# Batch 0's spatial product in three single-pass parts, with the opening's order written anew

## The chip, the cores and the metric

The kernel runs on one core of a Trainium2 chip. The metric is the device time of one execution in microseconds (us), the median of several. The core's engines run side by side, each through its own instructions in order: TensorE (in the profile PE, its weight loads PEld) multiplies matrices, VectorE (DVE) and ScalarE (ACT) work element by element, GpSimd (POOL) fills constants and issues a few transfers, SyncE (SP) issues nearly all transfers. An instruction waits at its engine's head until semaphores say that its operands are there and its target is free; everything behind it on that engine waits too.

## What is computed

Eight batches go through a linear attention with RMS norm, and its result through a gated block:

```python
kv = np.einsum('bhsd,bhse->bhde', k, v)            # B, H, S, D = 8, 8, 576, 64
out = np.einsum('bhsd,bhde->bhse', q, kv)
rms = np.sqrt(np.mean(out * out, axis=-1, keepdims=True) + 1e-06)
x = (out / rms * g_norm)                           # laid out as (B, 576, 512)
h = np.maximum(x @ w_in, 0.0)                      # w_in 512 x 1024
u, v = (h[..., :d_ff // 2], h[..., d_ff // 2:])
v_n = (v - mu) / np.sqrt(var + 1e-06)              # mean and variance over the 512 columns
v_s = np.einsum('ts,bsd->btd', w_spatial, v_n) + b_spatial[None, :, None]
return ((u * v_s) @ w_out).astype(np.float32)
```

All of it is in fp32. The product with `w_spatial` (576 x 576) is called the spatial product here.

## The kernel before

The 576 rows of a batch are four chunks of 128 (`NC`) and a tail of 64 (`TAIL`). Heads go in four pairs, so that a pair fills 128 partitions.

**Two ways to multiply.** A plain fp32 matmul is one instruction in the program and two records in the profile. From batch 1 on, an operand is held as a high part (a cast to fp32r by ScalarE) and a low part (the rest, a subtraction by VectorE); a product is then three fp32r matmuls, high by high, high by low, low by high (`hl`, `split`). Batches 1 to 7 also use seven products of quadrants instead of eight, for which sums of the quadrants of `w_spatial` lie ready in high and low parts (`WSH`, `WSL`, seven pieces for each of two row chunks).

**The opening.** Batch 0 starts while the weights still come in, and uses plain fp32: `hv_32` (v from `x` and `w_in`), `hv_tail_32` (the same for the tails of batches 0 and 1 together), `u_32` (u) and `sp_32`, the spatial product. `sp_32` makes eight units, four blocks of 128 columns by two halves of 288 rows; a unit sums over the four chunks and the tail, and VectorE multiplies the result into `U`. Meanwhile VectorE and ScalarE decode the float64 weights (`weight64_a` and `weight64_b`, five VectorE instructions for a 128x512 piece), split them (`split_in`, `split_ws`, `split_tail`, `split_out`), and TensorE already does batch 1's attention.

**What sets the order.** The string `PLAN` names the opening's steps, letter by letter: `W` the next weight load, `L` the next load of keys or queries, `c` and `C` the two halves of a decode, `J`, `K` the products of keys and values (instructions `pskv`), `A` and `D` queries (`pso`) and the norm's squares, `D` with ScalarE's accumulator, `A` with a VectorE reduction, `B` and `T` the norm's end and the transposes (`pstr`), `H` one step of `hv_32`, `e` and `F` relu and norm of v, `h` `hv_tail_32`, `u` u, `s` one unit of the spatial product, `X`, `E`, `z`, `O` the splits. Between `[` and `]` the order on PE, ACT and SP is pinned; behind that a scheduler orders the steps by its own timeline, in about the string's order. From the first `hv` of batch 1 (instructions `psh<-WVH,XH`) the program is written out in functions, `first`, `second` and `last` for each batch.

**Transfers.** SP issues in order; a transfer waits for the eighth before it, and for its buffer. Two key buffers (`KV0`, `KV1`) and two query buffers serve all pairs. The third and fourth piece of `w_out` come through one staging buffer: the third follows the stores of the first two split pieces (`spare_o<-WO`), the fourth the stores of the third.

Of the kernel before, what the change touches and what calls it, by code (L numbers as in the profile page):

```python
# [49 lines left out]
def body(ctx: ExitStack, tc, qT, kvm, kvt, g2, w_in, wsT, bsp, w_out, out):  # L50
# [275 lines left out]
    def split(hi, lo, x):  # L326
        nc.scalar.copy(hi, x)  # L327
        nc.vector.tensor_tensor(lo, x, f32(hi), op=ALU.subtract)  # L328
# [52 lines left out]
    def hv_tail_32():  # L381
        ps = ps_mm.tile([P, 512], F32, name="psh", tag="mm")
        for k in range(NP):
            nc.tensor.matmul(ps, X32[:, k, NT:XC], W32[k], start=k == 0, stop=k == NP - 1)
# [4 lines left out]
        d = work.tile([P, HS], F32, name="d", tag="g")[:, 0:HF]  # L389
        nc.vector.tensor_tensor(d[own], v[own, 0:HF], v[own, HF:FH], op=ALU.subtract)  # L390
        for x, cols in (v, slice(0, FH)), (d, slice(FH, FH + HF)):
            hi = TA[1][own, cols]
# [2 lines left out]
            nc.vector.tensor_tensor(TA[1][other, cols], x[own], f32(hi), op=ALU.subtract)

    def u_32(j, k):
        cols = slice(j * HS, (j + 1) * HS)
# [5 lines left out]
            if k == NP - 1:  # L404
                nc.scalar.activation(U[:, d, cols], psu[d], AF.Relu)

    def sp_32(d, j):
        ps = ps_mm.tile([P, 512], F32, name="psa", tag="mm")[:, 0:HS]
        ds, cols = slice(d * P, (d + 1) * P), slice(j * HS, (j + 1) * HS)
        for c in range(NC):  # L410
            nc.tensor.matmul(ps, V32[:, c, ds], staged["s", c][:, cols], start=c == 0, stop=False)  # L411
        nc.tensor.matmul(ps, VT32[0:TAIL + 1, ds], WT32[0:TAIL + 1, cols], start=False, stop=True)
# [334 lines left out]

    def blank_tails():
        nc.gpsimd.memset(VT32[TAIL:TAIL + 1], 1.0)
        for i in range(2):  # L750
            h = (1 - i) * TAIL
            nc.gpsimd.memset(f32(WTL[i][h:h + TAIL]), 0.0)
            nc.gpsimd.memset(f32(TB[i][h:h + TAIL]), 0.0)
            for r in (h, h + 32):
                nc.gpsimd.memset(f32(TB[i][r:r + 1, 0:FH]), 1.0)
# [267 lines left out]
```

## Time and profile before

| what | value |
|---|---|
| time, median of 3 runs (lowest to highest) | 512.27 us (512.09 to 512.9) |
| profiled execution: its time / its span | 511.49 us / 509.7 us |
| busy share of the span: PE, PEld, DVE, ACT, POOL | 98%, 86%, 81%, 57%, 4% |
| granted TensorE clock | 0.998 |
| DMA, mean over the span | 142 GB/s, 72.24 MB |

The span runs from the first to the last instruction. In rows of the timeline the first number is the start in us from the span's start, the second the duration of the row's whole group; `x8` counts instructions, and the bracket tells how long the engine had been idle and for whom it waited. Records of one engine overlap a little, since the next instruction starts while the last drains; the step from one start to the next is what an instruction costs in a dense stream. In rows of the chain of waits (the work that ended last, followed back) overlaps are taken off.

### The profile page before, as it was taken

The page shows a single profiled execution, that of the slowest core. Times are in us where ns is not written, and L with a number is a line of the kernel's source. Part 1 is how long each engine was busy: PE and PEld are TensorE (multiplying, and loading weights), DVE is VectorE, ACT ScalarE, POOL GpSimd, SP SyncE. Part 2 cuts the span into 40 slices and gives each one's busy share as a digit, 9 for nine tenths or more (in the row PEclk, how much of TensorE's full clock was granted, in tenths as well). Part 3 has the DMA queues.
Part 4 walks back from the last instruction along what each step waited for, and adds up shares of the span by engine and source line. Part 5 has one row for each costly group of instructions (what it writes and reads, how often), then busy time and mean ns, then how long its engine had stood idle before and what let it go on. Part 6 is the DMA issues. An engine that isn't in the chain of part 4 may idle for free.

```text
span 509.7 us, 9917 instructions
## 1 busy us (share of the span) xinstructions
PE 499.0 (98%) x3436; PEld 439.0 (86%) x3436; DVE 411.5 (81%) x1265; ACT 291.9 (57%) x1021; POOL 21.4 (4%) x47
## 2 busy tenths in 40 slices
PE   7999999999999999999999999999999999999996
PEld 6658788898988899989998899988998889988995
DVE  3898599688998699968897779968898579987860
ACT  2555456896734696457732688447642578527422
POOL 5000000000000001000000001000000001000000
PEclk9999999999999999999999999999999999999999
DMA  8995300735346516345265514424354511314223
GB/s 254 330 339 191 100 24 1 236 91 176 116 152 209 186 42 212 118 117 174 76 218 196 187 42 154 152 91 164 123 178 146 167 39 44 145 42 165 70 98 104
DMA packets 28071, 72.24 MB, mean 142 GB/s; under 512 B 3506, under 2 KB 8626, under 8 KB 26484
## 3 DMA queue, kind: packets, MB, share of 16 engines
q1 hardware_dynamic: 24564, 49.58, 29.9%
q0 software_dynamic: 3456, 22.02, 12.6%
q8 instruction: 27, 0.44, 0.4%
q14 instruction: 24, 0.20, 0.1%
HBM read 58.48 MB, written 13.11 MB: 140 GB/s over the span
## 4 chain that ended last, share of the span: by engine, by line
PE 78%; ACT 8%; DVE 7%; DMA 4%; POOL 1%; issue 1%; SPq 0%; ACTq 0%; POOLq 0%; DVEq 0%
PE pso L291 15%; PE psh L324 12%; PE psb L546 6%; PE psub L546 5%; PE pso L211 5%; PE psc L546 4%; PE pskv L136 3%; PE psa L546 3%; PE psua L546 3%; PE psuc L546 3%; PE psu L402 3%; PE psa L411 3%; PE psh L378 3%; PE pstr L239 2%; ACT x L194 2%; DMA out<-o 1%
## 5 line engine op out<-in xcount | busy, mean ns | idle before, releaser
L291 PE MATMUL pso<-WO,G 128*128 128x512 f32 x384 | 97.3, 396 | 0.0
L291 PEld LDWEIGHTS pso<-WO,G 128*128 128x128 f32 x384 | 70.3, 188 | 14.1
L327 ACT CAST G<-g 128x288 fp32r<-128x288 f32 (+1 forms) x56 | 22.8, 408 | 61.2 <-DVE g L567 60.8
L194 ACT ACTIVATE x<-pso 128x64 f32<-128x64 f32 x208 | 44.3, 252 | 5.5 <-PE pso L211 5.3
L324 PE MATMUL psh<-WVL,XH 128*128 128x512 f32 x112 | 43.7, 390 | 0.0
L324 PE MATMUL psh<-WVH,XH 128*128 128x512 f32 x112 | 43.6, 393 | 0.0
L194 ACT ACTIVATION_READ_ACCUMULATOR x<-pso 128x1 f32 x208 | 43.5, 238 | 0.0
L324 PE MATMUL psh<-WVH,XL 128*128 128x512 f32 x112 | 43.4, 392 | 0.0
L328 DVE TENSOR_TENSOR VL<-v,VH 128x512 fp32r<-128x512 f32 (+1 forms) x56 | 34.2, 619 | 7.8 <-ACT VH L327 7.6
L648 ACT COPY o<-pso 128x512 f32<-128x512 f32 x35 | 20.3, 593 | 26.0 <-PE pso L291 23.5
L327 ACT CAST VH<-v 128x512 fp32r<-128x512 f32 (+1 forms) x56 | 31.1, 574 | 4.2 <-DVE v L356 3.8
L303 DVE BATCH_NORM_STATS2 s<-v 128x6 f32<-128x512 f32 x32 | 21.8, 690 | 7.3 <-ACT v L297 7.1
L546 PE MATMUL psb<-WSH,VH 128*128 128x288 f32 x84 | 25.4, 304 | 0.2
L311 ACT ACTIVATE v<-v,mv,rv 128x512 f32<-128x512 f32 x28 | 23.2, 837 | 3.2 <-DVE mv L310 3.2
L324 PEld LDWEIGHTS psh<-WVH,XH 128*128 128x128 f32 x112 | 21.0, 188 | 4.6 <-ACT o L648 0.2
L297 ACT ACTIVATE v<-psh 128x512 f32<-128x512 f32 x32 | 18.7, 595 | 10.9 <-PE psh L324 7.6
L324 PEld LDWEIGHTS psh<-WVL,XH 128*128 128x128 f32 x112 | 21.0, 188 | 4.6
L324 PEld LDWEIGHTS psh<-WVH,XL 128*128 128x128 f32 x112 | 21.0, 188 | 4.4
L546 PE MATMUL psb<-WSL,VH 128*128 128x288 f32 x84 | 24.6, 295 | 0.0
L546 PE MATMUL psb<-WSH,VL 128*128 128x288 f32 x84 | 24.3, 297 | 0.1
L328 DVE TENSOR_TENSOR G<-g,G 128x288 fp32r<-128x288 f32 (+1 forms) x56 | 23.4, 418 | 1.1 <-ACT G L327 0.4
L136 PEld LDWEIGHTS pskv<-KV 128*64 128x64 f32 x512 | 18.1, 140 | 6.7 <-issue 2.9
(243 smaller groups left out, 1426.2 us busy)
## 6 DMA issues: line engine op xcount, KB each, us to landing
KV<-kvm SPq DMA_DIRECT2D x31, 512.0 KB, 5.1
WO<-spare_o POOLq DMA_DIRECT2D x12, 1024.0 KB, 6.6
UX<-spare_u POOLq DMA_DIRECT2D x12, 768.0 KB, 6.0
out<-o SPq DMA_DIRECT2D x32, 256.0 KB, 2.2
qt<-qT SPq DMA_DIRECT2D x16, 288.0 KB, 4.3
stage<-w_in SPq DMA_DIRECT2D x8, 512.0 KB, 6.4
qt<-qT SPq DMA_DIRECT2D x16, 256.0 KB, 2.9
KT<-kvt SPq DMA_DIRECT2D x32, 64.0 KB, 4.7
```

Of the source, the lines that this page charges most:

```text
L136: return nc.tensor.matmul(ps[h:h + D, at:at + D], of[:, 0, h:h + D], of[:, 1, h:h + D], start=c == 0, stop=c == NC)
L194: nc.scalar.activation(x[:, cols], ps[0:rows, cols], AF.Square, accum_out=ss[:, h:h + 1])
L211: nc.tensor.matmul(ps[:, c * P:(c + 1) * P], qt[:, c * P:(c + 1) * P], st[p], start=True, stop=True)
L291: nc.tensor.matmul(ps, lt, rh, start=i == 0, stop=i == n - 1)
L297: nc.scalar.activation(v, ps, AF.Relu)
L303: nc.vector.bn_stats(s6, v)
L311: nc.scalar.activation(v, v, AF.Identity, bias=m, scale=r)
L324: nc.tensor.matmul(ps, lt, rh, start=k == 0 and i == 0, stop=k == NP - 1 and i == 2)
L327: nc.scalar.copy(hi, x)
L328: nc.vector.tensor_tensor(lo, x, f32(hi), op=ALU.subtract)
L546: nc.tensor.matmul(ps, lt, rh, start=start and i == 0, stop=stop and i == len(pairs) - 1, skip_group_check=True)
L648: nc.scalar.copy(o, ps)
```

## The change

Batch 0's spatial product goes over to high and low parts. `sp_0` replaces `sp_32`: per chunk three fp32r matmuls with `WSH` and `WSL` instead of one in fp32, and the two matmuls of `tail_product` instead of one for the tail. `split_0` (letter `y`) splits the normalised v of batch 0, eight pieces of 128x256; `hv_tail_32` also splits batch 0's tail (`TA[0]`, `TB[0]`). The pieces of `w_spatial` must now be there before the units: `split_ws` (`E`) splits the four raw quadrants of a chunk pair, and the sums move behind the units, as `sums_ws` (`Y`); piece 6 holds a raw quadrant first and its sum later. One of the four norms of v multiplies on ScalarE (`f`). `PLAN` is new.

```diff
 PLAN = """
-[ W N8 G L c W C J00 L A00 L c L C n6 W J01 A01 J02 B00 T00 W A02 c H00 H20 J03 B01 T01 H30 B02 D03
-W T02 H31 c c W H10 C c W H11 H21 H32 H22 B03 H01 C c C W T03 H02 H12 H33 c H03 H13 L H23 e0 L | W C
-C L L a0 C e1 ] e2 e3 F1 L u00 F2 u01 K10 W Z F0 L A10 b0 L F3 t0 u02 u03 K12 u10 d1 b1 B10 A11 W
-u11 | | | t1 W u12 X3 W W A12 X2 Q0 h u13 s s L B12 T10 E0 s s B11 X0 E1 D13 s s X1 X5 W B13 T12 T11
-s X7 Q1 s T13 z P O1 p X4 X6 O0 W R
+[ L W N8 J00 L c G C D00 W n6 L W J01 c D01 B00 C J02 T00 L A02 H00 c B01 H30 H20 J03 T01 W B02 A03
+W T02 H10 W c c H31 C B03 L H21 L W H01 H22 C a0 H11 H32 C c H02 W W T03 C c H23 H33 H12 ] H03 e0
+H13 b0 L e1 C K10 F1 L L e2 W c e3 u00 C F2 f0 L t0 y1 y2 u01 F3 y0 A10 W K12 u02 X3 a1 Z u03 L y3
+u10 b1 X2 B10 t1 W A11 E0 u11 W L E1 W Q0 z u12 h D12 u13 s B12 s T10 X1 s | W s T12 X0 B11 D13 X5
+B13 s T11 X7 s s s Y1 Y0 X4 P T13 O0 Q1 W X6 p O1 R
 """
...
-        nc.scalar.copy(VT32[0:TAIL], v[0:TAIL])
-        own, other = slice(TAIL, P), slice(0, TAIL)
-        for x, cols in (v, slice(0, FH)), (d, slice(FH, FH + HF)):
-            hi = TA[1][own, cols]
+        for i, x, cols in (0, v, slice(0, FH)), (1, v, slice(0, FH)), (1, d, slice(FH, FH + HF)):
+            own, other = slice(i * TAIL, (i + 1) * TAIL), slice((1 - i) * TAIL, (2 - i) * TAIL)
+            hi = TA[i][own, cols]
             nc.scalar.copy(hi, x[own])
-            nc.scalar.copy(TB[1][own, cols], x[own])
-            nc.vector.tensor_tensor(TA[1][other, cols], x[own], f32(hi), op=ALU.subtract)
+            nc.scalar.copy(TB[i][own, cols], x[own])
+            nc.vector.tensor_tensor(TA[i][other, cols], x[own], f32(hi), op=ALU.subtract)
...
+    def split_0(c):
+        for i in range(2):
+            own = slice(i * HF, (i + 1) * HF)
+            name = ("p1", "u2", "u3", "g")[c]
+            hi0[c, i] = work.tile([P, HS], F32R, name=f"hi{name}", tag=name)[:, 0:HF]
+            split(hi0[c, i], V0L[:, c, own], raw[c][:, own])
...
-        for c in range(NC):
-            nc.tensor.matmul(ps, V32[:, c, ds], staged["s", c][:, cols], start=c == 0, stop=False)
-        nc.tensor.matmul(ps, VT32[0:TAIL + 1, ds], WT32[0:TAIL + 1, cols], start=False, stop=True)
+        cols, own = slice(j * HS, (j + 1) * HS), slice(d % 2 * P, (d % 2 + 1) * P)
+        multiply(ps, [m for c in range(NC) for m in
+                      hl(hi0[c, d // 2][:, own], V0L[:, c, d * P:(d + 1) * P],
+                         *(w[:, c % 2, (0, 6, 1, 2)[c // 2 * 2 + j]] for w in (WSH, WSL)))], True, False)
+        tail_product(ps, 0, d, j)
         nc.vector.tensor_tensor(U[:, d, cols], ps, U[:, d, cols], op=ALU.mult)
...
     def split_ws(k):
+        keep, b11, b12, b21, b22, _, _ = parts_ws(k)
+        for n, of in (0, b11), (1, b21), (2, b22), (6, b12):
+            keep(n, of)
+
+    def sums_ws(k):
+        keep, b11, b12, b21, b22, x, y = parts_ws(k)
         tc.keep_in_program_order(nc.vector.tensor_tensor(x, b12, b11, op=ALU.subtract))
         nc.vector.tensor_tensor(y, b22, x, op=ALU.subtract)
-        for n, of in enumerate((b11, b21, b22, x, y)):
-            keep(n, of)
+        keep(3, x)
+        keep(4, y)
```

Counted over the program, PE has 72 more matmuls of 128x288 (8 x 4 chunks x 3 and 8 x 2 tails instead of 8 x 5) and nothing else; behind the first `hv` of batch 1 its order is the same. DVE has eight more subtractions of 128x256, two of 128x288 and one of 64x512, and one reduction and one 128x512 scaling fewer. ACT has eight more casts of 128x256, two of 128x288, two of 64x512, and eight more squares of 128x64; one 64x512 copy is gone.

What moves, at three places. First SP at the program's start, before:

```order
L668 DMA stage<-w_in 128x1024
L900 DMA gcol<-g 128x1
L116 DMA KV_104<-kvm 128x2x256 x2
L117 DMA KT_106<-kvt 64x256
L126 DMA qt<-qT 128x576
```

and in the changed kernel:

```order
L115 DMA KV_104<-kvm 128x2x256 x2
L116 DMA KT_106<-kvt 64x256
L125 DMA qt<-qT 128x576
L682 DMA stage<-w_in 128x1024
L115 DMA KV_105<-kvm 128x1024
```

The first keys go ahead of the first weights. Second, PE where the spatial product begins (`psa` is a unit's bank, `pso` a query product, `psh<-RL,RH` the tails' v, `pstr` transposes of batch 1), before:

```order
L249 MATMUL pstt<-ident,x 128x128 x4
L211 MATMUL pso<-KVO_103,qt 128x128 x4
L384 MATMUL psh<-RL,RH 128x512 x4
L411 MATMUL psa<-stage,V_123 128x288 x8
L239 MATMUL pstr<-ident,x 128x128 x4
```

and in the changed kernel:

```order
L210 MATMUL pso<-KVO_102,qt 128x128 x4
L210 MATMUL pso<-KVO_103,qt 128x128 x4
L383 MATMUL psh<-RL,RH 128x512 x4
L238 MATMUL pstr<-ident,x 128x128 x4
L560 MATMUL psa<-WSH,hip_599 128x288
L560 MATMUL psa<-WSL,hip_599 128x288
```

The units now read `WSH`, `WSL`, the high parts `hi...` and `V0L` in place of the raw `stage` and `V`; batch 1's last query product and two groups of transposes, which lay among the units, follow them. Third, DVE ahead of the norms of batch 1's v (`BN_STATS`), before:

```order
L708 TENSOR_TENSOR WSL<-stage,WSH 128x288
L328 TENSOR_TENSOR WO<-stage,WO 128x512
L708 TENSOR_TENSOR WUL<-RL,WUH 128x2x256
L708 TENSOR_TENSOR WUL<-RL,WUH 128x512
L328 TENSOR_TENSOR WO<-stage,WO 128x512
L233 SCALAR_TENSOR_TENSOR XL<-pstr,gcol,XH 128x512
L762 TENSOR_TENSOR WTL_87<-WT_124,WTH 64x576
```

and in the changed kernel:

```order
L232 SCALAR_TENSOR_TENSOR XL<-pstr,gcol,XH 128x512
L722 TENSOR_TENSOR WSL<-stage,WSH 128x288
L152 COPY KVB<-pskv 64x2x64
L766 TENSOR_TENSOR stage<-stage 128x288
L722 TENSOR_TENSOR WSL<-stage,WSH 128x288
L722 TENSOR_TENSOR WUL<-RL,WUH 128x2x256
L327 TENSOR_TENSOR WO<-stage,WO 128x512 x2
```

The first two pieces of `w_out` are split last, behind the last of batch 1's x (`XL`) and the sums; the tails of `w_spatial` (`WTL`, `WTH`) are split early, before the units.

More of the change, by code (lines that the diff above doesn't have):

```diff
@@ L386, in hv_tail_32, with relu_0 @@
         layer_norm(ps, v, nc.vector)
-        nc.scalar.copy(VT32[0:TAIL], v[0:TAIL])
-        own, other = slice(TAIL, P), slice(0, TAIL)
-        d = work.tile([P, HS], F32, name="d", tag="g")[:, 0:HF]
-        nc.vector.tensor_tensor(d[own], v[own, 0:HF], v[own, HF:FH], op=ALU.subtract)
-        for x, cols in (v, slice(0, FH)), (d, slice(FH, FH + HF)):
-            hi = TA[1][own, cols]
-            nc.scalar.copy(hi, x[own])
-            nc.scalar.copy(TB[1][own, cols], x[own])
-            nc.vector.tensor_tensor(TA[1][other, cols], x[own], f32(hi), op=ALU.subtract)
+        d = work.tile([P, 512], F32, name="x", tag="x")[:, 0:HF]
+        last = slice(TAIL, P)
+        nc.vector.tensor_tensor(d[last], v[last, 0:HF], v[last, HF:FH], op=ALU.subtract)
+        for i, x, cols in (0, v, slice(0, FH)), (1, v, slice(0, FH)), (1, d, slice(FH, FH + HF)):
+            own, other = slice(i * TAIL, (i + 1) * TAIL), slice((1 - i) * TAIL, (2 - i) * TAIL)
+            hi = TA[i][own, cols]
+            nc.scalar.copy(hi, x[own])
+            nc.scalar.copy(TB[i][own, cols], x[own])
+            nc.vector.tensor_tensor(TA[i][other, cols], x[own], f32(hi), op=ALU.subtract)
+    raw, hi0 = {}, {}
+    def relu_0(c):
+        raw[c] = work.tile([P, FH], F32, name="v", tag="v", bufs=3) if c < NC - 1 else \
+            R[0][:, NP * XC:NP * XC + FH]
+        nc.scalar.activation(raw[c], psv[c], AF.Relu)
+    def split_0(c):
[4 more added lines that the diff above has]
+            split(hi0[c, i], V0L[:, c, own], raw[c][:, own])
     def u_32(j, k):
@@ L661, in body @@
     stage1 = staging[1].enter_context(tc.tile_pool(name="stage1", bufs=4, side="right"))
-    V32 = stage0.tile([P, NC, FH], F32, name="V32", tag="V32", bufs=1)
+    V0L = stage0.tile([P, NC, FH], F32R, name="V0L", tag="V0L", bufs=1)
     WT32 = stage0.tile([P, S], F32, name="WT32", tag="WT32", bufs=1)
@@ L728, in split_out, with parts_ws, split_ws @@
             nc.sync.dma_start(spare_o[:, i, k], f32(WO[:, i, k]))
-    def split_ws(k):
+    def parts_ws(k):
         t, t2 = staged["s", k], staged["s", k + 2]
-        b11, b12, b21, b22 = t[:, 0:HS], t[:, HS:S], t2[:, 0:HS], t2[:, HS:S]
-        x, y = t[:, S:S + HS], t2[:, S:S + HS]
         def keep(n, of):
             split_w(WSH[:, k, n], WSL[:, k, n], of)
+        return keep, t[:, 0:HS], t[:, HS:S], t2[:, 0:HS], t2[:, HS:S], t[:, S:S + HS], t2[:, S:S + HS]
+    def split_ws(k):
+        keep, b11, b12, b21, b22, _, _ = parts_ws(k)
[3 more added lines that the diff above has]
+        keep, b11, b12, b21, b22, x, y = parts_ws(k)
         tc.keep_in_program_order(nc.vector.tensor_tensor(x, b12, b11, op=ALU.subtract))
         nc.vector.tensor_tensor(y, b22, x, op=ALU.subtract)
-        for n, of in enumerate((b11, b21, b22, x, y)):
-            keep(n, of)
+        keep(3, x)
+        keep(4, y)
         nc.vector.tensor_tensor(x, b22, b12, op=ALU.subtract)
@@ L897, in body @@
         "t": lambda b: att_tail(b, st[b]),
-        "H": hv_32, "e": lambda c: nc.scalar.activation(V32[:, c], psv[c], AF.Relu),
-        "F": lambda c: normalize(V32[:, c], nc.vector),
+        "H": hv_32, "e": relu_0, "y": split_0, "Y": sums_ws,
+        "F": lambda c: normalize(raw[c], nc.vector), "f": lambda c: normalize(raw[c], nc.scalar),
         "G": lambda: nc.sync.dma_start(gcol, g2), "h": hv_tail_32, "u": u_32,
-        "s": lambda: sp_32(*units.pop(0)), "X": split_in, "E": split_ws, "z": split_tail,
+        "s": lambda: sp_0(*units.pop(0)), "X": split_in, "E": split_ws, "z": split_tail,
         "Z": blank_tails, "P": outw, "p": gates, "Q": make_out, "O": split_out, "R": split_g,
```

5 lines of the change are left out of this document (1 added, 4 removed).

## The prediction

> **What bounds the kernel now.** I read the page's busy shares first, then the busy time by stretches of 10 us through the opening, then TensorE's timeline, then the chain of waits.
>
> ```profile
> PE 499.0 (98%) x3436; PEld 439.0 (86%) x3436; DVE 411.5 (81%) x1265; ACT 291.9 (57%) x1021; POOL 21.4 (4%) x47
> PE 78%; ACT 8%; DVE 7%; DMA 4%; POOL 1%; issue 1%; SPq 0%; ACTq 0%; POOLq 0%; DVEq 0%
> ```
>
> TensorE is busy in 98% of the span and makes 78% of the chain. A busy share can hide waits, so the opening needs a closer look (columns: length, then busy us of PE, PEld, DVE, ACT, POOL, granted clock, DMA share, GB/s):
>
> ```profile
> 20.00:30.00 10.00, 10.00 (x56) 5.76 (x55) 8.40 (x23) 5.71 (x25) 0.00 (x0) 1.00 1.01 363
> 30.00:40.00 10.00, 10.00 (x72) 6.02 (x71) 10.00 (x23) 6.50 (x13) 0.00 (x0) 1.00 0.95 321
> 40.00:50.00 10.00, 10.00 (x82) 8.08 (x80) 9.03 (x41) 5.00 (x15) 0.00 (x0) 1.00 0.43 159
> 50.00:60.00 10.00, 9.84 (x53) 8.02 (x52) 3.12 (x12) 5.16 (x25) 0.00 (x0) 1.00 0.42 127
> 60.00:70.00 10.00, 10.00 (x39) 6.84 (x38) 9.66 (x25) 3.85 (x10) 0.00 (x0) 1.00 0.09 29
> 70.00:80.00 10.00, 10.00 (x47) 7.98 (x47) 9.86 (x30) 4.32 (x11) 0.00 (x0) 1.00 0.10 32
> 80.00:90.00 10.00, 10.00 (x49) 8.13 (x48) 9.67 (x26) 7.96 (x31) 0.00 (x0) 1.00 0.00 0
> 90.00:100.00 10.00, 9.85 (x88) 8.21 (x87) 6.41 (x12) 8.57 (x16) 0.00 (x0) 1.00 0.70 247
> ```
>
> From 20 to 100 us TensorE lacks 0.31 us of 80. VectorE sums to 66.2 us and is nearly full from 60 to 90; ScalarE sums to 47.1. TensorE's timeline gives the marks:
>
> ```profile
> 1.06 3.79 PE L805 MATMUL psw<-KVB 128*128 128x128 f32 x16 [1.06 <-DVE epsc L792]
> 6.35 0.69 PE L136 MATMUL pskv<-KV 128*64 128x64 f32 x8 [1.50 <-DMA KV<-kvm]
> 8.77 2.08 PE L211 MATMUL pso<-KVB,qt 128*128 128x128 f32 x8 [0.60 <-ACT KVB L154]
> 14.73 1.16 PE L211 MATMUL pso<-KVB,qt 128*128 128x128 f32 x8 [0.54 <-ACT KVB L154]
> 17.96 1.16 PE L211 MATMUL pso<-KVB,qt 128*128 128x128 f32 x8 [0.53 <-ACT KVB L154]
> 19.18 1.88 PE L378 MATMUL psh<-RL,RH 128*128 128x512 f32 x4
> 59.54 3.70 PE L384 MATMUL psh<-RL,RH 128*128 128x512 f32 x8 [0.16 <-ACT RH L253]
> 97.91 1.16 PE L211 MATMUL pso<-KVB,qt 128*128 128x128 f32 x8
> ```
>
> Up to 19 us it waits for keys and for ScalarE's copies; from 19.18 to 97.9 its only gap is the 0.16 us at 59.54. So time taken off its stream there comes off the span, if its operands keep up.
>
> **The product itself.** Rows of the chain of waits, overlaps taken off:
>
> ```profile
> 63.24 3.88 PE psa L411 x16
> 71.44 1.94 PE psa L412 x8
> 198.19 0.80 PE psa L546 x6
> 154.03 0.13 PE psc L552
> 84.86 8.20 PE psh L324 x36
> ```
>
> A record of the old product steps 3.88 / 16 = 0.2425 us, chunk and tail alike, and there are 64 + 16 = 80 of them, two for each of 40 matmuls: 19.4 us. The new matmuls have the form of batch 1's: 0.80 / 6 = 0.133 us each, and 0.13 for one of the tail. 8 x 4 x 3 + 8 x 2 = 112 of them take 14.9 us. **Term 1: -4.5 us.** The same shape runs at 0.133 us all through the later batches, so I give this +-0.2.
>
> By the Trainium skill, page "TensorE: Matmul & The Clock Gate", section "Back-to-back issue gap", an isolated matmul costs its columns over 2.4 GHz plus 2.5 ns: 122.5 ns here, and 5.9 us would be saved (32 x 122.5 ns, plus 8 x 2 x 122.5). The old records agree (two such to 0.2425 us), the fp32r rows stand at 133 and decide.
>
> **The first keys ahead of the first weights.** SP's issues, then the chain's way into the first query product:
>
> ```profile
> 0.75 0.39 SPq L668 DMA_DIRECT2D stage<-w_in  x1
> 1.66 1.33 SPq L116 DMA_DIRECT2D KV<-kvm  x2
> 7.75 0.53 POOL TB L755
> 8.28 0.20 ACT KVB L153
> 107.50 0.82 ACT x L194 x8
> ```
>
> The keys' issue comes 0.9 us earlier, and 512 KB of weights no longer go ahead of it (1.6 us at the 321 GB/s of the stretch from 30 us). The first keys, which landed at 6.3, are then there before the filler matmuls end at 4.85, so TensorE can start them 1.5 us earlier, and the product at 8.77 follows. Against it stands the norm: the first two query products now take ScalarE's accumulator, eight squares in 1.65 us (four, each with its read of the accumulator, make the row of 0.82) instead of one square and a VectorE reduction (some 1.3), and the copies that the third query product waits for (17.96) stand behind the second set. That costs 0.4 at most, and I count it whole. **Term 2: -1.1 us.** Bounds: -1.9, if the keys' second half and the query gain all of 2.3; and -0.1, if the copy at 8.28 really waits for POOL's last fill, as the chain has it (the keys' product ends at almost the same moment), because POOL loses just one fill of 0.5. I take the keys, since the other copies start as soon as their product ends. The gap at 59.54 goes too, because a query product now lies between (-0.2).
>
> **What VectorE and ScalarE must do more.**
>
> ```profile
> 55.50 0.17 DVE L174 TENSOR_SCALAR ah<-ss 128x8 f32<-128x8 f32 x1 [6.47 <-ACT x L194]
> 71.60 0.69 DVE L395 TENSOR_TENSOR TA<-v,TA 64x512 fp32r<-64x512 f32 x1
> 82.48 1.93 DVE L708 TENSOR_TENSOR WSL<-stage,WSH 128x288 fp32r<-128x288 f32 x5
> 114.69 0.41 DVE L328 TENSOR_TENSOR VL<-v,VH 128x256 fp32r<-128x256 f32 x1
> 113.98 0.41 ACT L327 CAST VH<-v 128x256 fp32r<-128x256 f32 x1
> ```
>
> VectorE: 8 x 0.41 + 2 x 0.39 + 0.69, less a reduction and a scaling of 128x512 (0.69 at most each): +3.4 to +3.6 us. ScalarE: 8 x 0.41, 2 x 0.4, two casts of 64x512 less a copy of that size (0.6), 1.65 for the squares: +6.3. Cover: the stretch from 20 us to the end of batch 1's `hv` shrinks from 80 to about 74; VectorE needs 66.2 + 3.6 = 69.8 of it, ScalarE 47.1 + 6.3 = 53.4. That fits, because the order fills VectorE's hole before 55.5: the first piece of `w_out`, the tails of `w_spatial` and the parts of v stand there now. But a slack of 4 us in 74 leaves local waits, and two can be named.
>
> First, the tail's parts. A unit ends with its tail; the first four units need 4 x 12 x 0.133 = 6.4 us, so with the transposes ahead (0.45) the low part of the tail is due 6.85 us after `h` ends. Before, `h` ended at 63.24 and that subtraction at 72.29: 9.05 us. By the new order there stand between them ScalarE's relu behind eight `WSH` casts, and on VectorE the statistics, two subtractions of 128x512, the small norm steps at 0.17, the scaling and the subtraction: some 6 us: 0.6, 0.7, 2 x 0.7, eight small ones with their hand-overs 2, 0.55, 0.7. Bounds 0 and 2.2 us; **term 3: +0.6**, near the new order's sum, with the banks: the fifth unit takes the first unit's bank, whose multiplication stands behind both tail subtractions.
>
> Second, `w_out`. The split of its first two pieces goes behind batch 1's last x, and the third piece's load (95.02 before) behind their stores:
>
> ```profile
> 95.02 0.42 SPq L668 DMA_DIRECT2D stage<-w_out  x1
> 112.28 5.10 DMA stage<-w_out
> 124.11 0.04 DVE WO L328
> 126.45 3.01 PE L291 MATMUL pso<-WO,G 128*128 128x512 f32 x12
> ```
>
> The fourth piece is split by 124.8, 1.65 us before TensorE takes it. TensorE arrives over 5 us earlier; the third load moves only some 2.5 us up, since VectorE's work behind the last x (six subtractions and a copy, 3.2 us) now lies ahead of it. If the whole chain moved by that, TensorE would wait 5.8 - 2.5 - 1.65 = 1.7 us; but between third load and fourth lie ScalarE's and VectorE's queues for batch 0's splits and batch 1's v, which do move with TensorE, and the third load (5.1 us like the fourth) landed by 101, while ScalarE is still busy with those. Bounds 0 and 1.7; **term 4: +0.2.**
>
> Sum: -4.5 - 1.1 - 0.2 + 0.6 + 0.2 = **-5.0 us**. Made on the profiled execution, 511.49 becomes 506.5; that run lies 0.8 below the median of the runs shown, 512.27, which becomes **507.3**. Behind 98 us TensorE's order is unchanged and it stays in front nearly everywhere, so the gain should last to the end.
>
> **Rivals.**
>
> *VectorE takes back half.* Where it is full, TensorE already waits for it:
>
> ```profile
> 144.68 0.63 PE L249 MATMUL pstt<-ident,x 128*128 128x128 f32 x4 [0.59 <-DVE x L203]
> ```
>
> If the tail's parts cost the full 2.2, the `w_out` chain its 1.7, and waits like this one grow, the gain is 5.8 - 3.9 - (up to 1) = 1 to 2.5 us: 510 to 511. For it: 9.7 of 10 us busy for thirty us, plus 3.6. Against: the hole of 6.5 us. Chance 0.2.
>
> *TensorE's slow start ends sooner.* Eight records of a query product took 2.08 us at 8.77 and 1.16 at 14.73, fillers 3.79 / 16 = 0.24 us each, at a granted clock shown as 1.00. The stretch became fast after running without a gap from 8.77 on. If closing the gap before 6.35 brings that on by one group, product and fillers (4.3 us together) take half: another -2 us, 505.3. By the Trainium skill, same page, section "What's actually happening", a gate halves the clock until a free-running window of about 3.4 us was busy; its phase is not mine to set. Chance 0.1.
>
> *Slower: the last weights come late.* The decodes feed `hv` and u:
>
> ```profile
> 42.38 0.66 DVE L703 TENSOR_TENSOR RH<-stage 128x512 f32<-128x512 f32 x1
> 44.45 2.10 PE L402 MATMUL psu<-RH 128*128 128x288 f32 x8
> ```
>
> The eighth decode ended 1.4 us before its use. Its load now follows two key loads and small ones, 1.5 MB, 4.6 us at 321 GB/s, on a DMA that is full (share 0.95 to 1.01). If it had landed only just before its decode, which takes some 7 us with what lies between, it would be late by 4.6 - 1.4, and as TensorE comes 1.1 us sooner, by 4.3; queued behind key buffers that TensorE frees later, more. From 5.8 us on it makes the kernel slower: 513 to 514. Against: in the old order the load was issued by 20.5, 20 us ahead. Chance 0.06.
>
> *Nothing much changes* (within 1 us): all bounds at once, or the new product not running as batch 1's does. Chance 0.05.
>
> **Numbers.** The forecast's chance is 0.59, its own range (terms 2 to 4 at their likely ends) 505.7 to 508.5. With the first two rivals inside, the range is **505.3 to 510.3**. 0.2% is 1.0 us, about what this measurement can tell: faster 0.59 + 0.2 + 0.1 = 0.89, less 0.01 for the first rival's edge beyond 511.3, 0.88; same 0.06; slower 0.06.
>
> **What would show it.** Right: records on the lines of `multiply` and `tail_product` in the opening, 112 in some 15 to 16 us; first keys' product near 4.9 and first `hv` step near 18.0; the query product that stood at 97.9 at 92 to 93; span near 504.7. Wrong: gaps at the first tail product or in front of batch 0's output with VectorE as releaser (first rival); the query product's eight records near 1.2 us (second); a wait of `psu` or `hv` on a decode, or on DMA, between 25 and 47 (third).

## The result, and the profile after

The changed kernel takes **505.72 us** (median of 4 runs, 505.06 to 506.31) against 512.28 us for the kernel before (512.09 to 512.9): ratio 0.987, 95% interval 0.9852 to 0.9887, so 6.6 us or 1.3% faster. Run again later beside other kernels it took 505.78 us, ratio 0.987 (0.9832 to 0.9907). The forecast was 507.3, its range 505.3 to 510.3. The profiled execution of the change took 506.31 us with a span of 504.5 us, 5.2 us under the span before.

The page's busy shares and the shares of the chain, after:

```profile
PE 491.7 (97%) x3468; PEld 436.2 (86%) x3468; DVE 413.4 (82%) x1275; ACT 296.9 (59%) x1048; POOL 20.6 (4%) x46
PE 81%; DVE 9%; DMA 4%; ACT 3%; issue 1%; SPq 1%; DVEq 0%; ACTq 0%
```

There are 32 TensorE records more (112 for 80) and 7.3 us less of TensorE's busy time. TensorE's timeline after, at the marks that the prediction used and at the new waits:

```profile
4.59 0.45 PE L135 MATMUL pskv<-KV 128*64 128x64 f32 x8
6.64 1.16 PE L210 MATMUL pso<-KVB,qt 128*128 128x128 f32 x8 [0.57 <-ACT KVB L153]
11.68 0.69 PE L135 MATMUL pskv<-KV 128*64 128x64 f32 x16 [2.32 <-DMA KV<-kvm]
13.50 1.16 PE L210 MATMUL pso<-KVB,qt 128*128 128x128 f32 x8 [1.01 <-ACT KVB L153]
17.46 1.16 PE L210 MATMUL pso<-KVB,qt 128*128 128x128 f32 x8 [0.39 <-ACT KVB L153]
49.83 0.71 PE L163 MATMUL pst<-KVO,qs 128*128 128x128 f32 x4 [1.06 <-ACT KVO L153]
50.91 1.72 PE L415 MATMUL psu<-RH,RL 128*128 128x288 f32 x6 [0.37 <-ACT U L418]
94.62 1.05 PE L210 MATMUL pso<-KVB,qt 128*128 128x128 f32 x8
```

The first keys start early as forecast (4.59), the eight records of the first query product take 1.16 us where they took 2.08, and then TensorE waits 2.32 us for the second keys. At 50 us stands a stall of 1.43 us that the prediction did not have. ScalarE's first decode, which started at 4.45 before, waits for the first weights, and the first squares and the next copies stand behind it:

```profile
10.37 0.66 ACT L707 ACTIVATE t<-stage 128x512 f32<-128x512 f32 x1 [3.78 <-DMA stage<-w_in]
```

The first and the last record of the new product (the next row behind the last starts at 79.73):

```profile
64.79 0.38 PE L560 MATMUL psa<-WSH,hip 128*128 128x288 f32 x1
79.60 0.30 PE L568 MATMUL psa<-WTL,TB 128*128 128x288 f32 x1
```

So its 112 records take 14.9 us, 0.133 each, without a gap.

Three marks cut the program into stages that can be compared between kernels: the first `hv` step, the `hv` product of the tails (`h`), and the query product that stood at 97.9. Busy time of TensorE in the stretches between them and behind the last (columns: stretch, its length, busy us and records, granted clock, DMA share, GB/s), first the kernel before:

```profile
19.18:59.54 40.36, 40.20 (x261) 1.00 0.72 248
59.54:97.91 38.37, 38.22 (x201) 1.00 0.18 58
97.90:540.00 442.10, 405.82 (x2856) 1.00 0.38 124
```

the change:

```profile
18.67:61.00 42.33, 40.90 (x261) 1.00 0.69 233
61.00:94.62 33.62, 33.62 (x234) 1.00 0.15 47
94.60:540.00 445.40, 404.91 (x2857) 1.00 0.37 125
```

and the change in its second profiled execution (span 503.1 us):

```profile
17.56:59.25 41.69, 40.91 (x261) 1.00 0.71 241
59.25:92.89 33.64, 33.64 (x235) 1.00 0.16 45
92.87:540.00 447.13, 405.09 (x2857) 1.00 0.38 125
```

(The last stretches run past the span's end, so their length says nothing; from the mark to the end it is 411.8, 409.9 and 410.2 us.) The spatial product's stage is 4.7 us shorter and without a gap. The stage ahead of it is 1.3 to 2.0 us longer, for the same 261 records. The opening is 0.5 us shorter in one execution and 1.6 us in the other. And some 1.6 to 1.9 us are gained behind the last mark, where TensorE's order is the old one. Of the kernel before there is one profiled execution; the run with more filler, an edit at its very start alone, repeats its last three stages to 0.2 us. All kernels that ran, by these stages (us; spans and marks from one profiled execution each, the time is the median of all; the profiled execution of the old product lies 1.6 us above its median, that of the swapped buffers 1.7, that of the tail splits behind `h` 2.0):

| kernel | first `hv` at | to `h` | to query product | to the end | time |
|---|---|---|---|---|---|
| before | 19.18 | 40.36 | 38.37 | 411.8 | 512.28 |
| the change, two executions | 18.67, 17.56 | 42.33, 41.69 | 33.62, 33.64 | 409.9, 410.2 | 505.72, 505.78 |
| old product, new order | 18.79 | 41.68 | 38.01 | 417.8 | 516.53 |
| `w_out` buffers swapped | 18.87 | 41.80 | 33.79 | 413.9 | 508.50 |
| first weight first | 20.12 | 40.77 | 33.75 | 409.8 | 507.11 |
| squares first | 18.49 | 42.48 | 33.67 | 411.6 | 507.65 |
| tail splits behind `h` | 19.31 | 40.74 | 39.00 | 422.0 | 520.90 |
| before, tail splits early | 19.88 | 41.06 | order differs | | 521.22 |
| before, more filler | 19.25 | 40.36 | 38.42 | 412.0 | 511.61 |
| subtractions twice | 18.29 | 42.75 | 34.96 | 410.4 | 508.18 |
| tail splits named first | 18.22 | 40.37 | 38.83 | 410.6 | 509.89 |
| tail casts on GpSimd | 17.84 | 41.54 | 34.03 | 411.0 | 506.26 |
| tail splits on GpSimd | 18.41 | 44.62 | 33.66 | 410.4 | 508.79 |

The theory after the result: the product's stream is the gain (4.7 us); the opening gives what its transfers allow; the new stall comes from ScalarE's queue; and VectorE and ScalarE have otherwise just room for the new work. The rivals: the new order is the gain, not the product; and VectorE or ScalarE still have slack.

### The profile page after: what moved, and what is told of

Read it like the earlier page. It is cut to its first block, busy times and chain, and to the rows that moved or that the text cites. A ratio compares the mean times of both kernels' runs of the same rounds, so it can differ in the third digit from the quotient of the medians.

```text
span 504.5 us, 10007 instructions
## 1 busy us (share of the span) xinstructions
PE 491.7 (97%) x3468; PEld 436.2 (86%) x3468; DVE 413.4 (82%) x1275; ACT 296.9 (59%) x1048; POOL 20.6 (4%) x46
## 4 chain that ended last, share of the span: by engine, by line
PE 81%; DVE 9%; DMA 4%; ACT 3%; issue 1%; SPq 1%; DVEq 0%; ACTq 0%
PE pso L290 19%; PE psh L323 15%; PE psb L560 6%; PE psa L560 6%; PE psub L560 5%; PE pso L210 4%; PE psc L560 4%; PE psua L560 4%; PE psuc L560 3%; PE pskv L135 3%; DMA stage<-w_out 2%; PE pstr L238 2%; PE psh L290 2%; PE psu L415 2%; DMA stage<-w_in 2%
## 5 line engine op out<-in xcount | busy, mean ns | idle before, releaser
L193 ACT ACTIVATE x<-pso 128x64 f32<-128x64 f32 x224 | 47.7, 249 | 6.3 <-PE pso L210 5.2
L193 ACT ACTIVATION_READ_ACCUMULATOR x<-pso 128x1 f32 x224 | 46.7, 234 | 0.0
L302 DVE BATCH_NORM_STATS2 s<-v 128x6 f32<-128x512 f32 x35 | 23.7, 689 | 6.2 <-ACT v L296 6.0
L231 ACT ACTIVATE XH<-pstr,gcol 128x512 fp32r<-128x512 f32 x28 | 19.6, 699 | 8.5 <-PE pstr L238 8.0
```

What stands on the lines that cost most here:

```text
L193: nc.scalar.activation(x[:, cols], ps[0:rows, cols], AF.Square, accum_out=ss[:, h:h + 1])
L231: nc.scalar.activation(hi, ps, AF.Copy, scale=gcol)
L302: nc.vector.bn_stats(s6, v)
```

## The experiments

### The old product in the new order

```diff
-        "H": hv_32, "e": relu_0, "y": split_0, "Y": sums_ws,
+        "H": hv_32, "e": lambda c: nc.scalar.activation(V32[:, c], psv[c], AF.Relu), "y": lambda c: None, "Y": sums_ws,
...
-        tail_product(ps, 0, d, j)
+        for c in range(NC):
+            nc.tensor.matmul(ps, V32[:, c, ds], staged["s", c][:, cols], start=c == 0, stop=False)
+        nc.tensor.matmul(ps, VT32[0:TAIL + 1, ds], WT32[0:TAIL + 1, cols], start=False, stop=True)
```

> The changed kernel with batch 0's spatial product and its tail undone to plain fp32 (80 records, and the tail's tokens added as the old 65th row); the new written-out order, the first keys ahead of the first weights, the early w_spatial splits and the late quadrants' sums are kept. Theory (the product's stream is the gain): TensorE spends 80 x 0.2425 = 19.4 us there again in place of the 14.7 us measured, so about 505.7 + 4.5 = 510.2 us, at most 1 us under it for the VectorE and ScalarE work that also goes. Rival (the new order is the gain, and the product only fills time that TensorE would have waited): 505.5 to 507.5 us.

Measured: 516.53 us, ratio to before 1.0086 (1.0057 to 1.0114). The stage of the product is 38.01 us, 4.4 longer than in the change: the stream, with the splits that feed it, is worth what the theory says, and the new order does not make that stage faster. But the time is 6 us above the theory's. TensorE's rows show where:

```profile
108.13 0.63 PE L239 MATMUL pstr<-ident,x 128*128 128x128 f32 x4 [2.50 <-DVE av L174]
111.26 0.44 PE L291 MATMUL psu<-XL,WUH 128*128 128x288 f32 x1
111.50 0.44 PE L291 MATMUL psu<-XH,WUL 128*128 128x288 f32 x1
```

Behind the last mark (98.48) it waits 2.50 us for a norm on VectorE, and then runs slowly: 0.24 us from record to record at 111 us, where the same records step 0.133 elsewhere. More waits of 1.3, 1.0 and 0.7 us follow. So the new order without the new product is slower than the kernel before, and this loss does not lie in the opening: the scheduler also places everything behind `]` anew. (The new product in the old order was not tried.)

### The two `w_out` buffers swapped

```diff
-        load64(w_out[k * P:(k + 1) * P, :], 2 * NP + k, stage0 if k == 1 else stage2)
+        load64(w_out[k * P:(k + 1) * P, :], 2 * NP + k, stage0 if k == 0 else stage2)
```

ScalarE's and SyncE's rows of the change, from which the edit comes:

```profile
44.82 0.68 ACT L707 ACTIVATE t<-stage 128x512 f32<-128x512 f32 x1 [2.62 <-DMA stage<-w_out]
37.39 0.33 SPq L682 DMA_DIRECT2D stage<-w_out  x1
39.51 0.33 SPq L682 DMA_DIRECT2D stage<-w_out  x1
```

The piece that ScalarE decodes first is issued second, at 39.51 behind two query loads.

> The changed kernel with the two w_out pieces' buffers exchanged, so that the piece which ScalarE decodes first is also the one that SyncE issues first. Theory (ScalarE's 2.62 us wait for the w_out transfer at 44.8 us is what holds the KVO copies and the u activations behind it, and through them TensorE for 1.06 + 0.37 = 1.43 us at 49.8 to 50.9): both TensorE gaps are gone, the next landmark, the x7 group at 61.00 us, comes 1.2 to 1.5 us earlier, and the time is 504.2 to 504.8 us. Rival (ScalarE and VectorE are behind by then anyway, so that the gap only moves): the landmark comes earlier by under 0.5 us, or the query product at 94.6 us stays within 0.3 us; 505.4 to 506.2 us.

Measured: 508.50 us, ratio 0.9926 (0.9901 to 0.9951), 2.8 us above the change. Both gaps at 50 us are gone (the rows at 48.80 and 49.53 have no bracket), yet the stage up to `h`, 41.80 us, is about as long as in the change (42.33 and 41.69), since a later row waits for VectorE:

```profile
58.42 0.63 PE L248 MATMUL pstt<-ident,x 128*128 128x128 f32 x4 [0.86 <-DVE x L202]
```

The rival is right about the sum: a gap closed on ScalarE opened on VectorE. The further 3.7 to 4.0 us behind the last mark come with waits for ScalarE, VectorE and a key transfer in the other order that the scheduler made; this execution took 510.20 us, 1.7 above the median.

### The first weight first again, and the squares first

```diff
-[ L W N8 J00 L c G C D00 W n6 L W J01 c D01 B00 C J02 T00 L A02 H00 c B01 H30 H20 J03 T01 W B02 A03
+[ W L N8 J00 L c G C D00 W n6 L W J01 c D01 B00 C J02 T00 L A02 H00 c B01 H30 H20 J03 T01 W B02 A03
```

> The changed kernel with the first weights' load issued ahead of the first keys' load again; all else as in the change. Theory of the prediction (the early keys are worth 1.1 us less 0.4 us): the first query product moves from 6.64 to about 8.5 us and the first hv step from 18.67 to about 19.3 us, time 506.2 to 506.6 us. Rival (the opening is set by the second keys' and w_in's transfers, which were waited for 2.32 us at 11.68): the second keys land no later than now, the first hv step stays within 0.3 us of 18.67 us, 505.4 to 506.0 us. If TensorE becomes fast only after a stretch without a longer gap, the first query product's eight records take 2.1 us again here, as they did at 8.77 us before the change, and 1.2 us if it is only a matter of the time since the start.

Measured: 507.11 us, ratio 0.9904 (0.9866 to 0.9943). TensorE's rows, and one of ScalarE:

```profile
6.98 1.39 PE L135 MATMUL pskv<-KV 128*64 128x64 f32 x16 [2.13 <-DMA KV<-kvm]
9.24 2.08 PE L210 MATMUL pso<-KVB,qt 128*128 128x128 f32 x8 [0.57 <-ACT KVB L153]
20.12 2.74 PE L377 MATMUL psh<-RL,RH 128*128 128x512 f32 x6
60.89 3.60 PE L383 MATMUL psh<-RL,RH 128*128 128x512 f32 x8
44.17 0.26 ACT L152 COPY KVO<-pskv 64x128 f32<-64x128 f32 x1 [0.25 <-PE pskv L135]
```

At the first `hv` step the theory holds, even more than expected: 1.5 to 2.6 us later than in the change, and the first query product is back at 2.08 us. But `h` starts at 60.89, no later than in the change's first execution (61.00): the stage between takes only 40.77 us. The scheduler has placed ScalarE's steps anew, so that the `KVO` copies stand ahead of the casts of the tail and behind no wait for `w_out` (44.17, in the change 49.26), and of the stall at 50 us only 0.27 us are left. So this edit changed two things, and what the early keys alone are worth at the end stays open: the medians differ by 1.4 us, but the intervals of the two ratios overlap.

```diff
-[ L W N8 J00 L c G C D00 W n6 L W J01 c D01 B00 C J02 T00 L A02 H00 c B01 H30 H20 J03 T01 W B02 A03
+[ L W N8 J00 L c G C D00 W n6 L W J01 D01 c B00 C J02 T00 L A02 H00 c B01 H30 H20 J03 T01 W B02 A03
```

> The changed kernel with the second query product's squares on ScalarE ahead of the decode step that waits for the second w_in piece at 14.3 us. Theory (this wait gates the squares, the squares gate the third keys' copies, and these hold TensorE for 0.39 us at 17.46): that gap is gone, the first hv step comes 0.3 to 0.5 us earlier than 18.67 us, 505.2 to 505.5 us. Rival (the w_in piece's decode is itself what the first hv step needs, and comes later by the 1.7 us of squares): the first hv step comes at 18.7 to 20 us, 505.7 to 507 us.

Measured: 507.65 us, ratio 0.9899 (0.9856 to 0.9941). The first `hv` step at 18.49 us lies between the change's two executions: no effect that can be told. In this execution the first query product waited for its queries' transfer instead:

```profile
7.26 1.13 PE L210 MATMUL pso<-KVB,qt 128*128 128x128 f32 x8 [1.15 <-DMA qt<-qT]
```

Which transfer TensorE waits for in the opening differs from one execution to the next, and the first `hv` step with it: by 1.1 us between the two executions of the change.

### Where the tail of `w_spatial` is split

Between the `w_out` transfer and the copies that TensorE waits for, ScalarE does the casts of `split_tail` (2.7 us from 45.4). Two edits move that step in the string, one behind `h`, one a place ahead:

```diff
-u10 b1 X2 B10 t1 W A11 E0 u11 W L E1 W Q0 z u12 h D12 u13 s B12 s T10 X1 s | W s T12 X0 B11 D13 X5
+u10 b1 X2 B10 t1 W A11 E0 u11 W L E1 W Q0 u12 h z D12 u13 s B12 s T10 X1 s | W s T12 X0 B11 D13 X5
```

> The changed kernel with the splits of w_spatial's tail (ScalarE's casts to WTH and WTL, 45.4 to 48.1 us, and VectorE's two subtractions at 49.35) named behind the tail's hv product instead of ahead of it. Theory (what TensorE lost at 49.8 to 50.9 us was ScalarE's queue: 2.62 us of w_out transfer and then 2.7 us of these casts in front of the KVO copies and the u activations): both gaps go, the tail's hv product starts at 59.5 to 59.8 us instead of 61.0; the time falls by 0.5 to 1.4 us if nothing behind it gives it back. Rival (VectorE is the one that is full from 20 us on, 17 to 19.5 of every 20 us, so that a gap closed on one engine opens on another): the tail's hv product under 0.6 us earlier, or a new wait of the first spatial products for WTH or WTL between 64 and 75 us; time within 0.5 us of the changed kernel's or above it.

Measured: 520.90 us, ratio 1.0154 (1.01 to 1.0208).

```profile
72.20 0.80 PE L566 MATMUL psa<-WTH,TA 128*128 128x288 f32 x4 [1.76 <-ACT WTH L783]
74.53 0.98 PE L568 MATMUL psa<-WTL,TB 128*128 128x288 f32 x4 [1.54 <-DVE WTL L786]
109.85 1.09 PE L238 MATMUL pstr<-ident,x 128*128 128x128 f32 x4 [3.65 <-DVE ah L173]
```

The gaps at 50 us are gone, as the theory said; the rival's new wait is there too, for the very pieces that were moved, and a scheduler's order with a 3.65 us wait behind it. The other edit leaves TensorE's and SyncE's orders as they are in the change:

```diff
-u10 b1 X2 B10 t1 W A11 E0 u11 W L E1 W Q0 z u12 h D12 u13 s B12 s T10 X1 s | W s T12 X0 B11 D13 X5
+u10 b1 X2 B10 t1 W A11 E0 u11 W L E1 W z Q0 u12 h D12 u13 s B12 s T10 X1 s | W s T12 X0 B11 D13 X5
```

> The changed kernel with the splits of w_spatial's tail named one step earlier, which in the built program puts ScalarE's casts behind the eight w_spatial casts at 62.2 us instead of ahead of the KVO copies at 49.3 us; TensorE's and SyncE's orders are the changed kernel's to the row, unlike in the run that named them behind the tail's hv product. Theory (these 2.7 us of casts, behind the w_out transfer, are what holds TensorE 0.8 to 1.4 us at 48 to 51 us, and with TensorE's order kept the gain survives): no wait for KVO or U there, the tail's hv product 0.8 to 1.4 us closer to the first hv step (40.9 us behind it instead of 41.7 to 42.3), and 504.4 to 505.2 us unless the tail's first products wait. Rival (the casts only move into the way of the next user): psa waits for WTH, WTL or TA between 66 and 75 us by 1 us or more, and the time stays within 0.4 us of 505.8 us or goes above it.

Measured: 509.89 us, ratio 0.9962 (0.9949 to 0.9975). TensorE's rows, then a second view, by stretches: the stage up to `h`, then two of 5 us (columns as above):

```profile
58.59 3.60 PE L383 MATMUL psh<-RL,RH 128*128 128x512 f32 x8
71.70 0.40 PE L566 MATMUL psa<-WTH,TA 128*128 128x288 f32 x1 [2.73 <-DVE TA L394]
73.64 0.45 PE L560 MATMUL psa<-WSL,hip 128*128 128x288 f32 x1
73.88 0.45 PE L560 MATMUL psa<-WSH,V0L 128*128 128x288 f32 x1
```

```profile
18.22:58.59 40.37, 40.37 (x261) 1.00 0.74 250
70.00:75.00 5.00, 2.97 (x15) 0.85 0.01 3
75.00:80.00 5.00, 5.00 (x33) 0.81 0.00 0
```

This settles the stall: with the casts out of ScalarE's way nothing is waited for at 50 us, and `h` comes 40.37 us behind the first `hv` step, the 40.36 of the kernel before. So the stall is the whole excess of 1.3 to 2.0 us in this stage. The brackets show 0.8 to 1.4 of it; the rest, which the busy column counts (40.90 for 40.37 us, the same 261 records), arises at the same two gaps, where the record ahead no longer overlaps the next (0.16 us each) and the first group behind takes 0.1 us more. ScalarE still waits 2.31 us for the `w_out` transfer in this run, and TensorE does not notice: it takes the wait and the casts together to make the copies late. It also shows the price: the casts now stand ahead of the tail's parts, and the first tail product waits 2.73 us for them. The product's stage grows by 5.2 us, 3.06 of them waits; of the rest 14 records at 0.24 us instead of 0.133 make 1.5.

```diff
-u11 | | | t1 W u12 X3 W W A12 X2 Q0 h u13 s s L B12 T10 E0 s s B11 X0 E1 D13 s s X1 X5 W B13 T12 T11
-s X7 Q1 s T13 z P O1 p X4 X6 O0 W R
+u11 | | | t1 W u12 X3 W W A12 X2 Q0 z h u13 s s L B12 T10 E0 s s B11 X0 E1 D13 s s X1 X5 W B13 T12 T11
+s X7 Q1 s T13 P O1 p X4 X6 O0 W R
```

> The kernel before with one edit of its written order: the splits of w_spatial's tail named ahead of the tail's hv product (where the change has them) instead of behind the last quadrant products. Theory (1.8 of the 5.2 us that the change gained arose between 98 and 155 us, where the kernel before has these splits, 94 to 100 us, in its chain of waits; taking them away early is what gained it): 0.5 to 1.9 us under the kernel before, with fewer waits after 98 us. Rival (that late gain is VectorE's and ScalarE's other early work, or the planner's other order, not these splits): within 0.4 us of the kernel before, or slower.

Measured: 521.22 us, ratio 1.017 (1.0113 to 1.0227). In the kernel before, the early splits put a ScalarE cast that waits 3.05 us for VectorE's subtraction ahead of the tail's parts, and batch 0's product waits:

```profile
77.17 2.42 PE L412 MATMUL psa<-WT,RH 65*128 65x288 f32 x8 [3.45 <-ACT RH L387]
```

Neither the theory nor its rival can be read from this: the new wait covers whatever the early splits give later. Where the late gain comes from stays open.

### How much room VectorE has

```diff
             split(hi0[c, i], V0L[:, c, own], raw[c][:, own])
+            nc.vector.tensor_tensor(V0L[:, c, own], raw[c][:, own], f32(hi0[c, i]), op=ALU.subtract)
```

> The changed kernel in which VectorE does the eight subtractions that make batch 0's low parts twice (8 x 0.36 = 2.9 us more of VectorE work between 51 and 61 us; TensorE's order stays as it is but for a few products within the first spatial product). Theory of the prediction (VectorE has some 4 us of slack there): the tail's hv product and the second query product within 0.5 us of the changed kernel's (59.3 to 61.0 and 92.9 to 94.6 us), time 505.5 to 506.3 us. Rival (VectorE, busy 17 to 19.5 of every 20 us, takes it back): the first spatial products wait for V0L, the query product comes 1.5 to 2.9 us later, time 507.3 to 508.7 us.

Measured: 508.18 us, ratio 0.9927 (0.9912 to 0.9943): 2.4 us more for 2.9 us of work.

```profile
71.75 0.40 PE L567 MATMUL psa<-WTH,TA 128*128 128x288 f32 x1 [0.32 <-DVE TA L394]
73.40 0.40 PE L561 MATMUL psa<-WSH,hip 128*128 128x288 f32 x1 [0.32 <-DVE U L428]
```

The stage up to `h` is 0.4 to 1.1 us longer than in the change, the product's 1.3. The rival is right about the size, though TensorE waits for `TA` and `U` and not for `V0L`: of 2.9 us added at this place, about half a microsecond was free, not four.

### The casts on GpSimd

```diff
-        keep(nc.scalar.copy(WTH[rows], WT32[rows]))
+        keep(nc.gpsimd.tensor_copy(WTH[rows], WT32[rows]))
...
-        keep(nc.scalar.copy(WTL[1][other], f32(WTL[0][rows])))
+        keep(nc.gpsimd.tensor_copy(WTL[1][other], f32(WTL[0][rows])))
```

(and the other casts of the tail likewise)

> The changed kernel with the six casts of w_spatial's tail done by GpSimd, which is idle from 8 to 162 us, instead of ScalarE; TensorE's and SyncE's orders are the changed kernel's to the row, and VectorE keeps its two subtractions. Theory (the casts in ScalarE's queue hold TensorE 0.8 to 1.4 us at 48 to 51 us, and late tail parts cost 5 us when the casts are put behind the w_spatial casts): neither wait is there, the tail's hv product comes 40.4 us behind the first hv step instead of 41.7 to 42.3 us, the second query product 33.6 us behind that as in the change, and the time is 503.9 to 504.9 us, 0.9 to 1.9 us under the change. Rival (VectorE is the limit right behind ScalarE: its 2.9 us of added work cost 2.4 us): a wait on VectorE (x, V0L or TA) opens between 50 and 75 us and the time stays within 0.4 us of 505.8 us; GpSimd's casts may also take so long that psa waits for WTH or WTL.

Measured: 506.26 us, ratio 0.9895 (0.9879 to 0.9912): not better than the change. The stall at 50 us is gone and the tail's parts are in time, but GpSimd starts as soon as the tail of `w_spatial` has landed, at 18.5 us, in the middle of VectorE's decodes:

```profile
18.54 0.66 POOL L781 CAST WTH<-WT 64x576 fp32r<-64x576 f32 x1 [11.02 <-DMA WT<-wsT]
19.98 1.47 POOL L785 CAST WTL<-WT 1x576 fp32r<-1x576 f32 x2
20.10 0.82 DVE L713 TENSOR_SCALAR t<-t 128x512 uint32<-128x512 uint32 x1
20.84 0.62 DVE L179 TENSOR_TENSOR rh<-sh,qh 128x8 f32<-128x8 f32 x1
24.00 0.63 PE L238 MATMUL pstr<-ident,x 128*128 128x128 f32 x4 [0.78 <-DVE x L202]
```

The same two VectorE instructions in the change's second execution:

```profile
19.79 0.43 DVE L713 TENSOR_SCALAR t<-t 128x512 uint32<-128x512 uint32 x1
20.13 0.16 DVE L179 TENSOR_TENSOR rh<-sh,qh 128x8 f32<-128x8 f32 x1
```

0.82 for 0.43 and 0.62 for 0.16: VectorE's small step ends at 21.46, GpSimd's two casts at 21.45, and TensorE waits 0.78 us for what follows on VectorE.

```diff
-        keep(nc.vector.tensor_tensor(low, WT32[r:r + 1], f32(low), op=ALU.subtract))
+        keep(nc.gpsimd.tensor_tensor(low, WT32[r:r + 1], f32(low), op=ALU.subtract))
```

(and the other subtraction likewise)

> The run beside it with the two subtractions of w_spatial's tail (0.74 and 0.75 us on VectorE at 49.35 us) on GpSimd too. If VectorE is as near the edge as its added work showed (2.4 us lost for 2.9 us), taking 1.5 us off it gives up to 1.2 us more than the run beside it: 503.0 to 504.0 us. If VectorE only has no room for more but does not yet hold TensorE: within 0.4 us of the run beside it. If GpSimd's subtractions take VectorE's time, or are so slow that psa waits for WTL between 66 and 75 us: above it by what is waited.

Measured: 508.79 us, ratio 0.9942 (0.9919 to 0.9965). The work of 1.5 us taken off VectorE was paid with more than that: one of its 0.16 us steps took 1.36, and TensorE waited for the result, 2.66 us.

```profile
23.74 1.36 DVE L181 SCALAR_TENSOR_TENSOR rh<-qh,rh 128x8 f32<-128x8 f32 x1
26.45 1.09 PE L238 MATMUL pstr<-ident,x 128*128 128x128 f32 x4 [2.66 <-DVE x L202]
```

### The kernel before with more filler

```diff
-[ W N8 G L c W C J00 L A00 L c L C n6 W J01 A01 J02 B00 T00 W A02 c H00 H20 J03 B01 T01 H30 B02 D03
+[ W N8 N8 G L c W C J00 L A00 L c L C n6 W J01 A01 J02 B00 T00 W A02 c H00 H20 J03 B01 T01 H30 B02 D03
```

> The kernel before with eight more of the filler products at the start (16 in place of 8), so that TensorE has no gap between the filler and the first keys at 6.35 us. If TensorE turns fast after some microseconds of unbroken work, the first query product's eight records take 1.16 us in place of 2.08 us and the twelve products behind it 1.5 us in place of 2.40 us, and the first hv step comes by up to 1 us earlier than 19.18 us unless a transfer is waited for there; the second keys' transfer, waited for 2.32 us in the changed kernel, says that most of it is waited away: time 0 to 0.8 us under the kernel before. If the slow start is a matter of the time since the first instruction, the eight records stay at 2.08 us and the time is no shorter.

Measured: 511.61 us, ratio 0.998 (0.996 to 0.9999).

```profile
8.89 1.16 PE L211 MATMUL pso<-KVB,qt 128*128 128x128 f32 x8 [0.59 <-ACT KVB L154]
13.46 0.69 PE L136 MATMUL pskv<-KV 128*64 128x64 f32 x16 [1.85 <-DMA KV<-kvm]
19.25 1.88 PE L378 MATMUL psh<-RL,RH 128*128 128x512 f32 x4
```

Without the gap ahead of the keys TensorE is fast at once (1.16 for 2.08 us), and then waits 1.85 us for the second keys: the first `hv` step comes at 19.25, where it was at 19.18. So TensorE's pace is not what sets the opening; the transfers of the keys, with ScalarE's copies behind them, are.

## Why the prediction was right, and where it was not

**Term 1 (-4.5, the product).** Right: the 112 records take the 14.9 us that were forecast, the stage of 38.37 us became 33.62 and 33.64, -4.7, and undoing the product gave back 4.4 in the same stage. The alternative of 5.9 is excluded.

**Term 2 (-1.1, the first keys first).** The size is between the two executions (-0.5 and -1.6 at the first `hv` step); the working named the wrong limit. It let TensorE's early start carry through, less 0.4 for ScalarE's squares. In the runs TensorE starts early and turns fast early, the second rival's mechanism, and then waits for the second keys (2.32 and 1.44 us), the third (0.81 and 0.82) and ScalarE's copies (1.01 + 0.39 in the first execution, 0.84 + 0.24 in the second). The working counted 0.4 for these copies, for the squares alone. It left out that the first weights, now behind the keys, hold the first decode at the head of ScalarE's queue for 3.78 us (2.75 in the second execution), with squares and copies behind it. The second rival's extra 2 us never came, since a transfer ends the opening: the filler run shows it directly.

**The stage up to `h` (0 forecast, but for a gap of 0.16).** The step that failed: "That fits, because the order fills VectorE's hole before 55.5." It cost 1.3 to 2.0 us, all of it the stall behind ScalarE's queue: with the casts named first the stage is 40.37 us again. The sum of ScalarE's work (53 of 74 us) said nothing on this: what counted was a 2.62 us wait for a transfer at the head of its queue, with 2.7 us of casts behind it and TensorE's copies behind those.

**Term 3 (+0.6, the tail's parts).** 0 in both executions. It was close: 2.9 us more on VectorE bring the wait (0.32), casts in ScalarE's way make it 2.73. The slack of some 4 us from which it was argued is about half a microsecond.

**Term 4 (+0.2, `w_out`).** 0: nothing is waited for there. But the prediction put everything else behind the last mark at nothing ("the gain should last to the end"), and 1.6 to 1.9 us are gained there. By TensorE's busy time behind that mark, 0.9 us is less waiting (6.0 us idle before, 5.0 and 5.1 after) and 0.7 to 0.9 less busy time for the same records. The cause stays open: in the one run meant to find it, a new wait ahead covers it.

So the forecast, 1.6 us too high, has its largest term right to 0.2 us; the loss that it missed ahead of the product (1.3 to 2.0) and the gain that it missed behind it (1.6 to 1.9) nearly cancel, which is luck, and the 0.8 us of terms 3 and 4 were not paid. The first rival (VectorE takes back half) did not happen, but stands right at the edge: 2.9 us of added work on VectorE gives 2.4 back. The slower rival found nothing: no `psu` or `hv` waited for a late weight before 47 us; the late weight that counted was `w_out`, three microseconds behind that.

## What to carry to other kernels

A sum of busy time tells that work fits into a stage, not that it fits in an in-order queue: look for the instruction at the head that will wait for a transfer, and add that wait to the work that stands between it and what another engine needs; here the wait without that work cost TensorE nothing. Work added to an engine that is 90% busy should be tested by adding the same once more, since the first dose can be free and the second paid almost in full. Where a scheduler places what follows, a one-word edit is not a one-step experiment: compare stage by stage between fixed marks, not by the time alone.

## What the runs showed of the hardware

**A wait costs more than its length.** After some waits TensorE's records step 0.24 us instead of 0.133 for 3 us and more: from 73.4 to 76.8 in the run with the casts named first, behind waits of 2.73 and 0.33 us (the granted clock reads 0.85 and 0.81 there); from 108.7 to 112.2 with the old product, behind 2.50 us; and from 109.9 to 115.8 with the tail splits behind `h`, behind 3.65 us. The Trainium skill, page "TensorE: Matmul & The Clock Gate", section "What's actually happening", has a gate that halves the clock and opens again after a window of about 3.4 us of sustained work; the first two lengths agree with that, the third is longer, and the step grows 1.8 times. The same section asks an idle window of about 3.4 us to close it, and here waits of 2.50 us, or of 2.73 and 0.33, were enough. Shorter ones did it at times: behind a wait of 1.67 us eight records took 2.02 us instead of 1.16 (at 7.40 in the run with the casts on GpSimd), while in the change's first execution eight such records behind waits of 2.32 and 1.01 us took their 1.16. The clock's column read 1.00 for the slow opening of the kernel before: the step between records is the surer sign.

**GpSimd holds up VectorE.** Small steps of 0.16 us took 0.62 and 1.36 beside GpSimd's casts and subtractions. The Trainium skill, page "SBUF — State Buffer", section "SBUF: two separate sides", calls the port pair that the two share an exclusive lock, held for a whole instruction; the trace agrees, with VectorE's 0.62 ending where GpSimd's casts end (21.46 and 21.45). Not every VectorE step is held: in the run with the subtractions on GpSimd too, one of 128x512 at 22.26 kept its 0.68 us, and the two casts beside it took 1.90 us instead of 1.47. An idle GpSimd is therefore no free place for work beside a busy VectorE.
